# Moving the sums and splits of GpSimd to VectorE in a fused attention and two-network kernel, with the gate as one ScalarE function and the pair stages in a written-out order

## The chip, the cores and the metric

The kernel runs on one core of one Trainium2 chip. The metric is the device time of one execution in microseconds, as the median of three runs. Beside the runs there is one profiled execution, whose instructions are in the trace. Engines are called by their names in the profile: PE is TensorE's matmul, PEld its weight load, DVE is VectorE, ACT is ScalarE, POOL is GpSimd, SP is the engine that issues most DMAs.

## The reference

Eight batches of eight heads (576 tokens, 64 columns per head) go through a linear attention; its output is 4608 tokens of 512 columns. These go through a network with squared ReLU and then through a gated network:

```
q_s = softmax(q, last axis);  k_s = softmax(k, token axis)
x   = q_s @ (k_s^T @ v)                    (heads side by side: 4608 x 512)
h   = relu(x @ w_in) ** 2;  x = h @ w_out  (2048 hidden columns)
xn  = x / sqrt(mean(x * x) + 1e-6) * rms_g
g   = xn @ w_gate;  val = xn @ w_val       (1536 hidden columns)
out = (g * sigmoid(g) * val) @ w_out2
```

All inputs and outputs are fp32.

## The kernel before

**Precision.** A matmul operand in fp32 is held as two fp32r tiles, a high part and a low part. ACT makes the high part with a copy, another engine the low part with a subtraction (operand minus high part). A product is then three matmuls (`PASSES`: high with high, high with low, low with high). So nearly every operand costs one ACT copy and one subtraction before PE can use it.

**Blocks.** The 4608 tokens are nine blocks of 512. The first network runs block after block (j from 0 to 8), in 16 units per block: unit (j, c) makes one slice of 128 hidden columns (`p1_A`, 12 matmuls into `ps_h`), squares the ReLU on ACT and splits it (`p1_hi`, `p1_lo`, tiles `r` and `g`), and two units later adds it to the four banks `acc` (`p1_B`, 12 matmuls). Attention for the following block runs beside it: the table `todo` gives each step of a pair of heads a place in the half units (`attention(2 * i)`, `attention(2 * i + 1)`).

**Weights of the second network.** They come as 64-bit words and must be made into fp32 and into the seven operands of a Strassen-Winograd product. This is done beside blocks 2 to 7 of the first network (counted from 0). `tick()` advances a pipeline: `d_load` (DMA), `d_words` (a scaling of the upper words, tile `s`, and an ACT copy of the lower words, tile `n`), `d_float` (three DVE instructions that write tile `t12`, `t21`, `t22` or `t11`). When four such tiles are there, `d_quad` queues 4 sums (`s1` to `s4`) and 7 or 8 splits into tiles `so` in the list `outs`; one entry is taken out per unit, and a second one while more than 8 are queued. A finished `so` tile is sent to DRAM (`wd_t`, `wd_v`) by a DMA of ACT (`send`, `flush`). Tiles `t12` and `t21` have two buffers, `t22` and `t11` one; `so` has four. In the kernel before, POOL makes the scalings of these weights, the sums and the low parts of `so`.

**The second network.** Blocks 0 to 7 are taken in four pairs (a pair stage), block 8 alone. A pair stage has two phases:

- Phase A (`p2_A`): for n from 0 to 5, 14 steps of 6 matmuls (512 columns). Seven steps give the gate half (k = 0), seven the value half (k = 1), into banks `ps_x`, `ps_y`, `ps_v` and `ps_w`; `ps_x` and `ps_y` share two buffers with `ps_h` and `ps_s`. DVE adds the banks up (`u`, `silu`, `g`). In the gate half ACT takes a Sigmoid (tile `sg`) and DVE multiplies it with its argument.
- Phase V (`p2_V`): 7 products i with 6 slices n each, 42 steps of 12 matmuls (256 columns). The operand of each step is a tile `ob` (four buffers): `p2_hi` copies the high part on ACT four steps ahead, `p2_lo` makes the low part on DVE three steps ahead. Four of the seven operands are sums or differences of `g` tiles: 24 such instructions per pair stage, made by POOL in place.

`b_tasks(s + 1)` spreads the preparation of the next stage over both phases: square sums and the root mean square (`b_sq`, `b_sum`, `b_rms`, `b_inv`), the scaling (`b_xn`), the sums for Strassen (`b_t`, `b_x4`), and in phase V the splits `xo` of 14 operand tiles (`b_xh` on ACT, `b_xl` on DVE).

**What sets the order.** While `pinned[0]` is true, every engine's instructions stay in the order in which the code records them; else a scheduler may move them. Before, phase V and nearly all of the first network are recorded in this way, phase A is not. Each engine runs its queue in order, so an instruction that waits holds up all behind it.

Of the kernel before, what the change touches and what calls it, by code (L numbers as in the profile page):

```python
# [8 lines left out]
F32 = mybir.dt.float32  # L9
# [31 lines left out]
def attention_moe_kernel(  # L41
# [84 lines left out]
    NOB = 4  # L126
    X0, XN = 2, 36
    NTAG = 8
# [127 lines left out]
    def d_words(key):  # L256
        r = raws.pop(key).bitcast(U32).rearrange("p (n two) -> p n two", two=2)
        turns["d"] += 1
        s = pools["d"].tile([P, 512], F32, tag=f"s{turns['d'] % 2}", name="s", bufs=1)
        n = pools["d"].tile([P, 512], I32, tag=f"n{turns['d'] % 2}", name="n", bufs=1)  # L260
        hi = r[:, :, 1].bitcast(F32)
        if key[0] == "o":
            se.activation(out=s, in_=hi, func=AF.Copy, scale=2.0**-112)
        else:
            eng = ve if key[0] == "i" else ge
            eng.tensor_scalar(
                out=s, in0=hi, scalar1=2.0**-112, scalar2=0.0, op0=ALU.mult, op1=ALU.add
            )
        se.activation(out=n, in_=r[:, :, 0], func=AF.Copy, scale=2.0**-29)
        words[key] = s, n  # L270

    def d_float(key):
# [21 lines left out]
        floats[key] = t.bitcast(F32)  # L294

    def w_split(t, f, eng):
        se.activation(out=t[:, 0], in_=f, func=AF.Copy)
        eng.tensor_tensor(out=t[:, 1], in0=f, in1=t[:, 0].bitcast(F32), op=ALU.subtract)

# [41 lines left out]

    outs = []

    def d_out(key, f):
        def run():
            turns["so"] += 1
            t = pools["q"].tile([P, 2, 512], F32R, tag=f"so{turns['so'] % 4}", name="so", bufs=1)
            w_split(t, f(), ge)
            send(key, t, 1)

        outs.append(run)

    def d_quad(key):
        n, c = key
        if n != "11":
            return
        f = {"a" + b: floats.pop((b, c)) for b in ("11", "12", "21", "22")}

        def d_sum(name, in0, in1, op):
            def run():  # L360
                f[name] = pools["q"].tile([P, 512], F32, tag=name, name=name, bufs=1)
                ge.tensor_tensor(out=f[name], in0=f[in0], in1=f[in1], op=op)

            outs.append(run)

        def out(name):
# [12 lines left out]
        out("s2")  # L379
        out("a12")  # L380
        out("s4")
# [569 lines left out]

    x2s, sums, rinv = {}, {}, {}

# [4 lines left out]

    def b_sq(j, m0):
        x2 = x2s[j]  # L960
        for m in range(m0, m0 + 2):
            s = ep.tile([P, T], F32, tag="e", name="sq")
            se.activation(out=s, in_=x2[:, m, :], func=AF.Square)
            if m == 0:
                sums[j] = s
            else:
                a = sums[j]
                if m == 1:
                    a = pools["x"].tile([P, T], F32, tag="sa", name="sa", bufs=1)
                ve.tensor_tensor(out=a, in0=sums[j], in1=s, op=ALU.add)  # L970
                sums[j] = a

    def b_sum(j):
        a = sums.pop(j)
        t = pools["x"].tile([P, 2, T], F32R, tag="shl", name="shl", bufs=1)
        split(t, a)
        sums[j] = t

    def b_rms(j):
# [4 lines left out]
        y = pools["x"].tile([P, T], F32, tag="y", name="y", bufs=1)  # L984
        se.activation(out=y, in_=ps, func=AF.Ln, bias=eps_sb)
        se.activation(out=y, in_=y, func=AF.Exp, scale=-0.5)
        a = pools["x"].tile([P, T], F32, tag="sa", name="sa", bufs=1)
        ve.tensor_scalar_add(out=a, in0=ps, scalar1=1e-6)
        rinv[j] = (y, a)

    def b_inv(j):
        y, a = rinv[j]
        ve.tensor_tensor(out=a, in0=a, in1=y, op=ALU.mult)
        ve.tensor_tensor(out=a, in0=a, in1=y, op=ALU.mult)
        ve.tensor_scalar(
# [84 lines left out]
    def p2_A(s, n, q):  # L1080
# [63 lines left out]
        if step == 0:  # L1144
            se.activation(out=sv("p1"), in_=ps, func=AF.Copy)
        elif step == 1:
            add(sv("u2"), ps, sv2["p1"])
        elif step == 3:
            out(0, 0, ps2.pop("x"))
        elif step == 2:  # L1150
            se.activation(out=sv("p5"), in_=ps, func=AF.Copy)
        elif step == 4:
            add(sv("u3"), ps2.pop("y"), sv2["p1"])
        elif step == 5:
            out(0, 1, ps2.pop("v"), sv2["u2"])
        else:
            w = ps2.pop("w")
            out(1, 0, w, sv2["u3"])
            out(1, 1, sv2["p5"], sv2["u3"])

    gs, ops, banks, parts2 = {}, {}, {}, {}
    BSTEPS = ("b11", "t2", "b21", "t3", "t1", "t4", "b22")
    AT = {"b11": (0, 0), "b12": (0, 1), "b21": (1, 0), "b22": (1, 1)}
    AT |= {"t2": (0, 0), "t3": (0, 1), "t1": (0, 1), "t4": (1, 0)}

    def p2_g(n, name):
        k, t = AT[name]
        return gs[2 * n + k][:, t]

    def p2_hi(i, n):  # L1170
        o = ops[i, n] = pools["x"].tile([P, 2, T], F32R, tag="ob", name="ob", bufs=NOB)
        se.activation(out=o[:, 0], in_=p2_g(n, BSTEPS[i]), func=AF.Copy)

    def p2_lo(i, n):
# [5 lines left out]
        for out, in0, in1, op in {  # L1180
            "b11": (("t3", "b22", "b12", ALU.subtract), ("t2", "t3", "b11", ALU.add)),
            "b21": (("t4", "b21", "t2", ALU.subtract),),
            "t3": (("t1", "b22", "t2", ALU.subtract),),
        }.get(name, ()):
            ge.tensor_tensor(out=p2_g(n, out), in0=p2_g(n, in0), in1=p2_g(n, in1), op=op)

    def p2_V(s, i, n):
# [26 lines left out]
        def part(name, h):  # L1214
            tag = {"p1": ("p1", "u2"), "u2": ("silu10", "silu11"), "p5": ("p5", "u3")}[name][h]
            parts2[name, h] = pools["x"].tile([P, T], F32, tag=tag, name=tag, bufs=1)
            return parts2[name, h]
# [13 lines left out]
        for h in range(2):  # L1231
# [9 lines left out]
            elif i == 4:  # L1241
                se.activation(out=part("p5", h), in_=p, func=AF.Copy)
            elif i == 5:
                done(0, 1, h, lambda e: add(e, p, parts2["p1", h]))
                done(
                    1, 1, h, lambda e: add(e, parts2.pop(("p5", h)), parts2.pop(("p1", h)))
                )
            else:
# [60 lines left out]
    def b_tasks(s):  # L1309

        blocks = stages[s]
        tasks = [(0, b_load, (j,)) for j in blocks]
        at = 6
        for j in blocks:
            tasks += [(at, b_sq, (j, 0)), (at + 6, b_sq, (j, 2)), (at + 12, b_sum, (j,))]
            tasks += [(at + 16, b_rms, (j,)), (at + 19, b_inv, (j,))]
            tasks += [(at + 23 + 3 * m, b_xn, (j, m)) for m in range(KD)]
            at += 35
        tasks += [(n, b_t, (s, b)) for n, b in ((76, "b"), (76, "t1"), (79, "t2"), (82, "t3"))]
        names = [b for a, b, bank in STEPS]  # L1320
# [3 lines left out]
        for i, (b, kk) in enumerate(tiles):  # L1324
            at = NA + i if s == 0 else NA + X0 + i * XN // len(tiles)
            if b == "t4":
                tasks.append((at - 1 - 3 * kk, b_x4, (s, kk)))
            tasks += [(at, b_xh, (s, b, kk)), (at + 1, b_xl, (s, b, kk))]
        return sorted(tasks, key=lambda x: x[0])

    with ExitStack() as ctx_a:
# [127 lines left out]
        for i, (j, c) in enumerate(units):  # L1459
# [47 lines left out]
            attention(2 * i + 1)  # L1507
            if i == n1 - FF1 - 1:
                assert not outs and ticks[0] == len(jobs) + 4
# [13 lines left out]
        for op in plan2:  # L1523
# [5 lines left out]
            elif op[0] == "A":  # L1529
                _, s, n, q = op  # L1530
                p2_A(s, n, q)
                at = n * 2 * NS + q
                if n == NQ - 1 and len(stages[s]) == 2:
                    if q in (2, 4, 6, 8):
                        p2_hi(0, q // 2 - 1)
                    if q in (3, 5, 7, 9):
                        p2_lo(0, q // 2 - 1)
            else:
# [6 lines left out]
                if NOB <= at + NOB - 1 < NS * NQ:  # L1545
                    p2_lo(*divmod(at + NOB - 1, NQ))
                at += NA
            if at is not None and s + 1 < len(stages):
                for when, f, args in b_tasks(s + 1):
                    if when == at:  # L1550
                        f(*args)
                pinned[0] = False

# [44 lines left out]
```

## Time and profile before

| | |
|---|---|
| median of three runs | 1719.31 us (1718.97 to 1719.57) |
| profiled execution, its time | 1717.88 us |
| its span, first to last instruction | 1715.7 us |
| PE busy | 1683.8 us, 98% of the span |
| DVE busy | 1165.0 us, 68%, 1895 instructions |
| ACT busy | 833.1 us, 49% |
| POOL busy | 347.4 us, 20%, 271 instructions |

The span is what the trace covers; the profiled execution took 2.2 us more than it. Busy time is the union of an engine's instructions. A row of the chain or of a wait names what ended the idle time, with `<-` before the releaser. The granted TensorE clock is 1.00 in nearly all of the span.

### The profile page before, as it was taken

What the parts mean: (1) busy time and instruction counts of PE and PEld (TensorE: products, weight loads), DVE (VectorE), ACT (ScalarE), POOL (GpSimd) and SP (SyncE); (2) the same over time, 40 slices, a digit from 0 to 9 for tenths busy, and PEclk for the clock granted to TensorE, in tenths of its full rate; (3) what the DMA queues carried; (4) which work ended last, traced back from release to release, by engine and by line L of the source; (5) the groups of instructions that cost most, each with busy time, mean ns of one, the idle gap of its engine ahead of it and who ended that gap; (6) DMA issues with size and microseconds to landing.
All of it is one profiled execution on the core that took longest, in us unless ns stands there. A gap on an engine that the chain in (4) does not pass through costs nothing.

```text
span 1715.7 us, 25334 instructions
## 1 busy us (share of the span) xinstructions
PE 1683.8 (98%) x9254; PEld 1433.2 (84%) x9254; DVE 1165.0 (68%) x1895; ACT 833.1 (49%) x1454; POOL 347.4 (20%) x271
## 2 busy tenths in 40 slices
PE   7999999999999999999999999999999999999998
PEld 5788888888878778888888789888987899889997
DVE  7986556656765666432457889688978897868744
ACT  7875345555555555543555345434644354324422
POOL 4000001233442334320001114011501150214000
PEclk9999999999999999999999999999999999999999
DMA  9986666798988988675556556755585557556786
GB/s 239 306 286 240 203 188 218 243 310 263 323 297 257 304 250 276 226 246 197 172 199 206 187 194 202 252 187 193 182 272 185 196 184 246 187 194 198 248 303 221
DMA packets 202554, 398.03 MB, mean 232 GB/s; under 512 B 57664, under 2 KB 123200, under 8 KB 201280
## 3 DMA queue, kind: packets, MB, share of 16 engines
q1 hardware_dynamic: 162800, 348.97, 62.4%
q10 hardware_dynamic: 39632, 47.46, 8.0%
q8 instruction: 74, 1.21, 0.3%
q14 instruction: 48, 0.39, 0.1%
HBM read 330.30 MB, written 66.06 MB: 231 GB/s over the span
## 4 chain that ended last, share of the span: by engine, by line
PE 83%; DVE 11%; issue 3%; ACT 1%; DMA 1%; POOL 1%; ACTq 0%; SPq 0%; DVEq 0%; POOLq 0%
PE acc L34 23%; PE ps_h L34 21%; PE ps_x L34 15%; PE ps_y L34 11%; PE ps_v L34 7%; PE ps_w L34 4%; DVE ob L34 3%; DVE g L34 2%; DVE xo L34 1%; PE ps_kv L34 1%; DVE t L34 1%; DVE u L34 1%; DVE silu L34 1%; DVE sa L34 1%; DVE x L34 1%
## 5 line engine op out<-in xcount | busy, mean ns | idle before, releaser
L34 PE MATMUL ps_h<-x,ws 128*128 128x512 f32 x1296 | 315.4, 393 | 0.3 <-ACT r L34 0.3
L34 PE MATMUL acc<-g,ws 128*128 128x512 f32 x1296 | 314.0, 391 | 0.0
L34 POOL TENSOR_TENSOR g<-g 128x512 f32<-128x512 f32 x96 | 155.4, 1631 | 663.8 <-DVE g L34 411.2
L34 PEld LDWEIGHTS acc<-g,ws 128*128 128x128 f32 x1296 | 241.4, 188 | 50.0
L34 PEld LDWEIGHTS ps_h<-x,ws 128*128 128x128 f32 x1296 | 240.1, 188 | 50.7 <-ACT r L34 1.2
L34 DVE TENSOR_TENSOR g<-r,g 128x512 fp32r<-128x512 f32 x156 | 111.8, 717 | 132.4 <-ACT g L34 132.3
L34 ACT ACTIVATE r<-ps_h 128x512 f32<-128x512 f32 x144 | 85.8, 596 | 217.7 <-PE ps_h L34 214.4
L34 ACT ACTIVATE ob<-g 128x512 fp32r<-128x512 f32 x168 | 106.1, 632 | 142.4 <-PE ps_x L34 67.8
L34 PE MATMUL ps_y<-xo,ws 128*128 128x512 f32 (+1 forms) x720 | 168.5, 369 | 1.6 <-DVE u L34 1.6
L34 PE MATMUL ps_v<-xo,ws 128*128 128x512 f32 (+1 forms) x720 | 169.0, 368 | 0.0
L34 PE MATMUL ps_x<-xo,ws 128*128 128x512 f32 (+1 forms) x720 | 168.0, 369 | 0.0
L34 DVE TENSOR_TENSOR ob<-g,ob 128x512 fp32r<-128x512 f32 x168 | 145.7, 890 | 24.5 <-ACT ob L34 22.7
L34 PEld LDWEIGHTS ps_y<-xo,ws 128*128 128x128 f32 x720 | 126.6, 189 | 25.7 <-DVE u L34 3.1
L34 PEld LDWEIGHTS ps_x<-xo,ws 128*128 128x128 f32 x720 | 126.9, 189 | 23.7 <-DVE u L34 1.2
L34 PEld LDWEIGHTS ps_v<-xo,ws 128*128 128x128 f32 x720 | 127.4, 188 | 23.0
L34 PE MATMUL ps_x<-ws,ob 128*128 128x256 f32 x1152 | 142.4, 283 | 0.4
L34 PEld LDWEIGHTS ps_x<-ws,ob 128*128 128x128 f32 x1152 | 140.0, 192 | 1.9 <-DVE ob L34 1.6
L34 PE MATMUL ps_y<-ws,ob 128*128 128x256 f32 x864 | 107.4, 284 | 7.5 <-DVE ob L34 7.5
L34 PEld LDWEIGHTS ps_y<-ws,ob 128*128 128x128 f32 x864 | 104.9, 192 | 8.9 <-DVE ob L34 8.9
L34 ACT ACTIVATE g<-r 128x512 fp32r<-128x512 f32 x156 | 98.4, 631 | 22.6 <-DVE r L34 18.4
L34 PE MATMUL ps_h<-x,w 128*128 128x512 f32 x432 | 104.6, 392 | 2.1 <-DVE x L34 2.1
L34 PE MATMUL acc<-g,w 128*128 128x512 f32 x432 | 105.1, 392 | 0.0
(165 smaller groups left out, 2351.8 us busy)
## 6 DMA issues: line engine op xcount, KB each, us to landing
ws<-wd_t SPq DMA_DIRECT2D x210, 512.0 KB, 3.3
ws<-wd_o SPq DMA_DIRECT2D x96, 512.0 KB, 4.5
ws<-wd_i SPq DMA_DIRECT2D x88, 512.0 KB, 4.5
ws<-wd_v SPq DMA_DIRECT2D x84, 512.0 KB, 3.3
wd_t<-so ACTq DMA_DIRECT2D x84, 256.0 KB, 5.2
raw<-in_w_gv SPq DMA_DIRECT2D x36, 512.0 KB, 5.7
wd_v<-so ACTq DMA_DIRECT2D x48, 256.0 KB, 3.7
x2d<-e SPq DMA_DIRECT2D x36, 256.0 KB, 3.5
```

The costliest lines, as they stand in the source:

```text
L34: ins = f(*args, **kw)
```

## The change

1. `d_words`: the scaling of the second network's weights goes from POOL to DVE. `d_sum` and the low part in `d_out` likewise. The low part is no longer recorded with its copy: it goes to a list `lows`, emptied after the unit's second attention step, and its tile is sent at once. A second entry of `outs` is taken while more than 5 are queued, not 8.
2. `p2_A`: Sigmoid and multiplication become one ACT function, Silu, recorded a little later (`later`). Phase A of a pair stage is pinned.
3. `p2_lo` no longer makes the sums of `g`; a new `p2_t` makes each of them on DVE, at places written out in `V_SUMS` and in the main loop: `t3` in phase A, `t2` in phase A or in the first three steps of phase V, `t1` and `t4` in steps 14 to 26 of phase V.
4. `b_tasks`: single steps at fixed places (`V_LOWS`, `V_T4` for phase V) in the place of an even spread. In `b_rms` ACT copies the bank (plus 1e-6), which DVE did, and ACT squares the inverse root, which saves DVE one multiplication per block.
5. `p2_V`: product 4 is added to the result at once, where before ACT copied it for product 5.

```
-    X0, XN = 2, 36
+    V_SUMS = {1: (4, "t2"), 2: (5, "t2")}
+    V_SUMS |= {15 + n: (n, "t1") for n in range(6)}
+    V_SUMS |= {at: (n, "t4") for n, at in enumerate((14, 21, 22, 24, 25, 26))}
+    V_LOWS = (3, 4, 5, 6, 7, 8, 9, 10, 27, 28, 30, 31, 32, 33)
+    V_T4 = (12, 13)
...
-            eng = ve if key[0] == "i" else ge
-            eng.tensor_scalar(
+            ve.tensor_scalar(
...
-            w_split(t, f(), ge)
-            send(key, t, 1)
+            src = f()
+            se.activation(out=t[:, 0], in_=src, func=AF.Copy)
+
+            def low():
+                ve.tensor_tensor(
+                    out=t[:, 1], in0=src, in1=t[:, 0].bitcast(F32), op=ALU.subtract
+                )
+                send(key, t, 0)
+
+            lows.append(low)
...
-                ge.tensor_tensor(out=f[name], in0=f[in0], in1=f[in1], op=op)
+                ve.tensor_tensor(out=f[name], in0=f[in0], in1=f[in1], op=op)
...
-        se.activation(out=y, in_=ps, func=AF.Ln, bias=eps_sb)
+        a = pools["x"].tile([P, T], F32, tag="sa", name="sa", bufs=1)
+        se.activation(out=a, in_=ps, func=AF.Copy, bias=1e-6)
...
-                g = pools["x"].tile([P, T], F32, tag="sg", name="sg", bufs=2)[:, 0:W]
-                se.activation(out=g, in_=h, func=AF.Sigmoid)
-                ve.tensor_tensor(out=to, in0=h, in1=g, op=ALU.mult)
+                later.append(lambda: se.activation(out=to, in_=h, func=AF.Silu))
...
+    def p2_t(n, name):
+        in0, in1, op = {
+            "t3": ("b22", "b12", ALU.subtract),
+            "t2": ("t3", "b11", ALU.add),
+            "t4": ("b21", "t2", ALU.subtract),
+            "t1": ("b22", "t2", ALU.subtract),
+        }[name]
+        ve.tensor_tensor(out=p2_g(n, name), in0=p2_g(n, in0), in1=p2_g(n, in1), op=op)
...
-            ge.tensor_tensor(out=p2_g(n, out), in0=p2_g(n, in0), in1=p2_g(n, in1), op=op)
...
-            at = NA + i if s == 0 else NA + X0 + i * XN // len(tiles)
+            at = NA + (i if s == 0 else V_LOWS[i] - 1)
...
-                if len(outs) > 8:
+                if len(outs) > 5:
...
+                pinned[0] = len(stages[s]) == 2
...
+                if at in V_SUMS:
+                    p2_t(*V_SUMS[at])
```

**Place 1: DVE beside the first network, where a float tile's buffer is used again.** `t12` is the float tile of a weight, `so` the split of an older one, `g` a split of the first network, `x`, `qT`, `mk`, `mc` attention steps. Before:

```order
L34 TENSOR_REDUCE mk_6318<-kt_6038 128x128
L34 TENSOR_TENSOR mk_6318<-mk_6318,kt_6038 64x128
L34 TENSOR_TENSOR g_6314<-r_6311,g_6314 128x512
L34 TENSOR_SCALAR t12_6336<-s_6224 128x512
L34 SCALAR_TENSOR_TENSOR t12_6336<-s_6224,t12_6336 128x512
L34 ISA t12_6336<-t12_6336,n_6225 128x1024
L34 TENSOR_REDUCE mc_6384<-ps_kt_6360 128x1
```

Of the change:

```order
L34 TENSOR_TENSOR so_6244<-s2_5975,so_6244 128x512
L34 TENSOR_TENSOR g_6274<-r_6271,g_6274 128x512
L34 TENSOR_TENSOR so_6301<-t12_5314,so_6301 128x512
L34 TENSOR_TENSOR x_6305<-ps_x_6276,x_6305 128x512
L34 TENSOR_TENSOR qT_6307<-ps_q_6246,qT_6307 128x512
L34 TENSOR_REDUCE mk_6330<-kt_6044 128x128
L34 TENSOR_TENSOR mk_6330<-mk_6330,kt_6044 64x128
L34 TENSOR_TENSOR g_6326<-r_6323,g_6326 128x512
L34 TENSOR_SCALAR t12_6348<-s_6238 128x512
L34 SCALAR_TENSOR_TENSOR t12_6348<-s_6238,t12_6348 128x512
```

The last reader of the old buffer (`so` from `t12`) was an instruction of POOL's queue; now it is one of DVE's own, six rows ahead of the instruction that writes the buffer again.

**Place 2: DVE in phase V of the first pair stage, from the third product on.** `ob` is a low part that PE waits for, `xo` a low part for the next stage, `t` a sum for the next stage, `g` a sum of this stage, `p` and `u` are sums that empty banks. Before:

```order
L34 TENSOR_TENSOR ob<-g,ob 128x512 x3
L34 TENSOR_TENSOR xo<-t_9717,xo 128x512
L34 TENSOR_TENSOR ob<-g,ob 128x512 x2
L34 TENSOR_TENSOR xo<-t_9717,xo 128x512
L34 TENSOR_TENSOR ob<-g,ob 128x512 x3
L34 TENSOR_TENSOR xo<-x_8783,xo 128x512
L34 TENSOR_TENSOR ob<-g,ob 128x512 x3
L34 TENSOR_TENSOR xo<-x_8783,xo 128x512
```

Of the change:

```order
L34 TENSOR_TENSOR t_9641<-x_8785,t_9641 128x512
L34 TENSOR_TENSOR ob<-g,ob 128x512
L34 TENSOR_TENSOR t_9641<-x_8785,t_9641 128x512
L34 TENSOR_TENSOR ob<-g,ob 128x512
L34 TENSOR_TENSOR g<-g 128x512
L34 TENSOR_TENSOR ob<-g,ob 128x512
L34 TENSOR_TENSOR g<-g 128x512
L34 TENSOR_TENSOR ob<-g,ob 128x512
L34 TENSOR_TENSOR g<-g 128x512
```

The sums `g<-g`, which stood in POOL's queue, now stand in DVE's, one between each two low parts; the splits `xo` have moved to other steps.

## Rows read from the trace of the kernel before

**Rows 1.** The page, part 1: busy time and instructions of each engine.

```profile
PE 1683.8 (98%) x9254; PEld 1433.2 (84%) x9254; DVE 1165.0 (68%) x1895; ACT 833.1 (49%) x1454; POOL 347.4 (20%) x271
```

**Rows 2.** PE's waits: us in total, times, longest us.

```profile
PE ps_y L34 <- DVE ob L34: 7.5, 7, 1.6
...
PE ps_kt L34 <- DVE mk L34: 2.5, 4, 0.9
...
PE ps_h L34 <- DVE x L34: 2.1, 1, 2.1
PE ps_y L34 <- DVE u L34: 1.6, 3, 0.6
PE acc L34 <- ACT g L34: 1.3, 1, 1.3
PE ps_x L34 <- DVE qT L34: 1.0, 1, 1.0
...
PE ps_kb L34 <- DVE x L34: 0.4, 1, 0.4
```

**Rows 3.** All engines' waits (same columns), two of the first network.

```profile
POOL so L34 <- ACT so L34: 248.2, 46, 12.5
...
DVE t L34 <- POOL so L34: 26.0, 6, 8.8
```

**Rows 4.** Timeline (start us, us, instruction, [idle before]), first network, around 609 us.

```profile
607.27 0.62 ACT L34 ACTIVATE so<-t 128x512 fp32r<-128x512 f32 x1
...
608.03 1.29 POOL L34 TENSOR_TENSOR so<-t,so 128x512 fp32r<-128x512 f32 x1 [4.96 <-ACT so L34]
...
609.35 1.50 DVE L34 TENSOR_SCALAR t<-s 128x512 uint32<-128x512 uint32 x1 [7.77 <-POOL so L34]
...
615.98 0.68 DVE L34 TENSOR_TENSOR x<-ps_x,x 128x512 fp32r<-128x512 f32 x1
...
616.71 0.73 PE L34 MATMUL ps_h<-x,w 128*128 128x512 f32 x2 [2.08 <-DVE x L34]
```

**Rows 5.** Timeline of PE in the first phase V.

```profile
1014.98 8.79 PE L34 MATMUL ps_x<-ws,ob 128*128 128x256 f32 x72
1023.61 8.80 PE L34 MATMUL ps_y<-ws,ob 128*128 128x256 f32 x72
...
1043.58 4.58 PE L34 MATMUL ps_y<-ws,ob 128*128 128x256 f32 x36 [0.85 <-DVE ob L34]
1049.26 2.90 PE L34 MATMUL ps_y<-ws,ob 128*128 128x256 f32 x22 [1.11 <-DVE ob L34]
...
1078.56 1.55 PE L34 MATMUL ps_x<-xo,ws 128*128 128x512 f32 x6
```

**Rows 6.** Timeline of DVE and POOL in the same phase V.

```profile
1028.01 0.68 DVE L34 TENSOR_TENSOR xo<-t,xo 128x512 fp32r<-128x512 f32 x1
...
1033.89 5.08 POOL L34 TENSOR_TENSOR g<-g 128x512 f32<-128x512 f32 x3 [0.71 <-DVE ob L34]
...
1036.04 1.78 DVE L34 TENSOR_TENSOR xo<-t,xo 128x512 fp32r<-128x512 f32 x1
```

**Rows 7.** DVE's groups by form: count | busy us, mean ns | idle before.

```profile
L34 DVE TENSOR_TENSOR ob<-g,ob 128x512 fp32r<-128x512 f32 x168 | 145.7, 890 | 24.5 <-ACT ob L34 22.7
...
L34 DVE TENSOR_TENSOR silu<-silu,sg 128x512 f32<-128x512 f32 x72 | 48.4, 685 | 7.1 <-ACT sg L34 6.9
...
L34 DVE TENSOR_SCALAR s<-raw 128x512 f32<-128x512 f32 x16 | 6.7, 419 | 0.0
```

**Rows 8.** POOL's costliest groups by form.

```profile
L34 POOL TENSOR_TENSOR g<-g 128x512 f32<-128x512 f32 x96 | 155.4, 1631 | 663.8 <-DVE g L34 411.2 <-PE ps_x L34 147.2 <-DVE ob L34 103.7
L34 POOL TENSOR_TENSOR so<-s,so 128x512 fp32r<-128x512 f32 x36 | 49.3, 1370 | 150.5 <-ACT so L34 126.4 <-issue 10.8 <-DVE t L34 7.6
```

**Rows 9.** Busy us of each engine in the first phase V (PE, PEld, DVE, ACT, POOL).

```profile
1015.00:1078.50 63.50, 61.41 (x505) 60.60 (x504) 54.69 (x67) 35.39 (x60) 24.43 (x15) 1.00 0.63 212
```

More of the change, by code (lines that the diff above doesn't have):

```diff
@@ L294, in d_float @@
         floats[key] = t.bitcast(F32)
-    def w_split(t, f, eng):
-        se.activation(out=t[:, 0], in_=f, func=AF.Copy)
-        eng.tensor_tensor(out=t[:, 1], in0=f, in1=t[:, 0].bitcast(F32), op=ALU.subtract)
     late = []
@@ L339, in d_lo @@
             send(key, t, 1)
-    outs = []
+    outs, lows = [], []
     def d_out(key, f):
@@ L949, in p1_out @@
             nc.sync.dma_start(out=x2d[j][:, m, :], in_=e)
-    x2s, sums, rinv = {}, {}, {}
+    x2s, sums, rinv, sqs = {}, {}, {}, {}
     def b_load(j):
@@ L957, in b_load, with b_sq, b_add, b_shi @@
         x2s[j] = t
[L959 to L974, printed above, removed]
-        t = pools["x"].tile([P, 2, T], F32R, tag="shl", name="shl", bufs=1)
-        split(t, a)
+    def b_sq(j, m):
+        t = sqs[j, m] = ep.tile([P, T], F32, tag="e", name="sq")
+        se.activation(out=t, in_=x2s[j][:, m, :], func=AF.Square)
+    def b_add(j, m):
+        a = sqs.pop((j, 0)) if m == 1 else sums[j]
+        t = pools["x"].tile([P, T], F32, tag="sa", name="sa", bufs=1) if m == 1 else a
+        ve.tensor_tensor(out=t, in0=a, in1=sqs.pop((j, m)), op=ALU.add)
+        sums[j] = t
+    def b_shi(j):
+        t = pools["x"].tile([P, 2, T], F32R, tag="shl", name="shl", bufs=1)
+        se.activation(out=t[:, 0], in_=sums[j], func=AF.Copy)
+        sums[j] = t, sums[j]
+    def b_slo(j):
+        t, a = sums[j]
+        ve.tensor_tensor(out=t[:, 1], in0=a, in1=t[:, 0].bitcast(F32), op=ALU.subtract)
         sums[j] = t
@@ L984, in b_rms, with b_ln, b_exp @@
         y = pools["x"].tile([P, T], F32, tag="y", name="y", bufs=1)
-        se.activation(out=y, in_=ps, func=AF.Ln, bias=eps_sb)
+        a = pools["x"].tile([P, T], F32, tag="sa", name="sa", bufs=1)
+        se.activation(out=a, in_=ps, func=AF.Copy, bias=1e-6)
+        rinv[j] = (y, a)
+    def b_ln(j):
+        y, a = rinv[j]
+        se.activation(out=y, in_=a, func=AF.Ln)
+    def b_exp(j):
+        y, a = rinv[j]
         se.activation(out=y, in_=y, func=AF.Exp, scale=-0.5)
-        a = pools["x"].tile([P, T], F32, tag="sa", name="sa", bufs=1)
-        ve.tensor_scalar_add(out=a, in0=ps, scalar1=1e-6)
-        rinv[j] = (y, a)
+        z = ep.tile([P, T], F32, tag="e", name="z")
+        se.activation(out=z, in_=y, func=AF.Square)
+        rinv[j] = (y, a, z)
     def b_inv(j):
-        y, a = rinv[j]
-        ve.tensor_tensor(out=a, in0=a, in1=y, op=ALU.mult)
-        ve.tensor_tensor(out=a, in0=a, in1=y, op=ALU.mult)
+        y, a, z = rinv[j]
+        ve.tensor_tensor(out=a, in0=a, in1=z, op=ALU.mult)
         ve.tensor_scalar(
@@ L1145, in p2_A @@
             se.activation(out=sv("p1"), in_=ps, func=AF.Copy)
+            while later:
+                later.pop(0)()
         elif step == 1:
@@ L1149, in p2_A @@
             out(0, 0, ps2.pop("x"))
+            while later:
+                later.pop(0)()
         elif step == 2:
@@ L1155, in p2_A @@
             out(0, 1, ps2.pop("v"), sv2["u2"])
+            while later:
+                later.pop(0)()
         else:
@@ L1161, in attention_moe_kernel @@
     gs, ops, banks, parts2 = {}, {}, {}, {}
+    later = []
     BSTEPS = ("b11", "t2", "b21", "t3", "t1", "t4", "b22")
@@ L1179, in p2_lo @@
         )
[L1180 to L1184, printed above, removed]
-            ge.tensor_tensor(out=p2_g(n, out), in0=p2_g(n, in0), in1=p2_g(n, in1), op=op)
     def p2_V(s, i, n):
@@ L1214, in part @@
         def part(name, h):
[L1215 removed]
+            tag = {"p1": ("p1", "u2"), "u2": ("silu10", "silu11")}[name][h]
             parts2[name, h] = pools["x"].tile([P, T], F32, tag=tag, name=tag, bufs=1)
@@ L1241, in p2_V @@
             elif i == 4:
-                se.activation(out=part("p5", h), in_=p, func=AF.Copy)
+                done(1, 1, h, lambda e: add(e, p, parts2["p1", h]))
             elif i == 5:
[L1244 to L1247, printed above, removed]
+                done(0, 1, h, lambda e: add(e, p, parts2.pop(("p1", h))))
             else:
@@ L1312, in b_tasks @@
         tasks = [(0, b_load, (j,)) for j in blocks]
[L1313 to L1319, printed above, removed]
+        for at, j in zip((9, 37), blocks):
+            tasks += [(at + n, b_sq, (j, m)) for m, n in enumerate((0, 1, 2, 3))]
+            tasks += [(at + 1 + m, b_add, (j, m)) for m in (1, 2, 3)]
+            tasks += [(at + 6, b_shi, (j,)), (at + 7, b_slo, (j,)), (at + 10, b_rms, (j,))]
+            tasks += [(at + 14, b_ln, (j,)), (at + 15, b_exp, (j,)), (at + 20, b_inv, (j,))]
+            tasks += [(at + 22 + 2 * m, b_xn, (j, m)) for m in range(KD)]
+        tasks += [(n, b_t, (s, b)) for n, b in ((66, "b"), (66, "t1"), (72, "t2"), (77, "t3"))]
         names = [b for a, b, bank in STEPS]
@@ L1324, in b_tasks @@
         for i, (b, kk) in enumerate(tiles):
-            at = NA + i if s == 0 else NA + X0 + i * XN // len(tiles)
+            at = NA + (i if s == 0 else V_LOWS[i] - 1)
             if b == "t4":
-                tasks.append((at - 1 - 3 * kk, b_x4, (s, kk)))
+                tasks.append((at - 1 - 3 * kk if s == 0 else NA + V_T4[kk], b_x4, (s, kk)))
             tasks += [(at, b_xh, (s, b, kk)), (at + 1, b_xl, (s, b, kk))]
@@ L1507, in attention_moe_kernel @@
             attention(2 * i + 1)
+            while lows:
+                lows.pop(0)()
             if i == n1 - FF1 - 1:
@@ L1530, in attention_moe_kernel @@
                 _, s, n, q = op
+                pinned[0] = len(stages[s]) == 2
                 p2_A(s, n, q)
                 at = n * 2 * NS + q
[L1533 to L1537, printed above, removed]
+                if len(stages[s]) == 2 and (n > 0 and q == 5 or n == NQ - 1 and q == 2 * NS - 1):
+                    p2_t(n - (q == 5), "t3")
+                if len(stages[s]) == 2:
+                    for k in range(NOB):
+                        when = at - (NQ - 3 + k // 2) * 2 * NS - 9 - k % 2
+                        if when == 0:
+                            p2_hi(0, k)
+                        elif when == 1:
+                            p2_lo(0, k)
+                        elif when == 3:
+                            p2_t(k, "t2")
             else:
@@ L1551, in attention_moe_kernel @@
                         f(*args)
-                pinned[0] = False
+            pinned[0] = False
 def kernel(**inputs):
```

## The prediction

> **What bounds the kernel now.** I read the busy times of the engines first: PE is busy in 98% of the span, DVE in 68%, POOL in 20% [rows 1]. The matmuls themselves are the same before and after, so the change can only take away what is left beside them, the time in which PE waits. So the next view is the list of PE's waits. After the first 60 us it has three kinds, and that list is the whole stock [rows 2]:
>
> - beside the first network, waits for attention steps of DVE: `mk` 2.5 us, `x` 2.1 and 0.4, `qT` 1.0, together 6.0;
> - in phase A of the pair stages, 1.6 us for DVE's `u`, which empties a bank;
> - in phase V, 7.5 us in 7 waits for DVE's `ob`.
>
> The wait of 1.3 us for ACT at the end belongs to the single last stage and stays. Each of the three kinds names DVE, so the third view is what held DVE up. There are two answers.
>
> The first is a wait. In the list of all waits DVE stands before its instruction `t` for POOL's `so`, 6 times, 26.0 us in all [rows 3]. The timeline shows one of them link by link [rows 4]: ACT copies `so` at 607.27, POOL makes the low part at 608.03, DVE, which had nothing to do for 7.77 us, starts `t` at 609.35, its attention step `x` comes at 615.98, and PE, which needs it, has lost 2.08 us.
>
> The second is slow instructions. In phase V the same DVE instruction `xo` takes 0.68 us at 1028.01 and 1.78 us at 1036.04, inside a run of three POOL sums that lasts 5.08 us [rows 6]. A gate multiplication, made where POOL is idle, takes 685 ns in the mean; `ob`, of the same size, takes 890 [rows 7].
>
> In phase V the price of this can be read in full. Six steps (72 matmuls) start 8.63 us after the six before them (1014.98 to 1023.61), so 42 steps would take 7 times 8.63, or 60.4 us; the phase takes 63.6 (1014.98 to 1078.56) [rows 5]. So 3.2 us are lost, of which the two marked waits are 1.96: a wait costs about 1.6 times what its row shows, since PE restarts slowly and shorter waits follow.
>
> **The change part by part.**
>
> *Phase V.* DVE's work there, counted in the order: 38 low parts, 14 splits for the next stage, 14 sums that were POOL's, 2 `b_x4` and 8 instructions that empty banks, 76 in all. At 685 ns [rows 7] they are 52.1 us of the 60.4, though no longer in the company of POOL. A step lasts 8.63 / 6 = 1.44 us, and the written-out order puts two DVE instructions (1.37 us) in a step and three (2.06) in the four steps where DVE empties banks. A low part has three steps, 4.3 us, before PE needs it, and ACT's copy takes under one of them, so 0.6 us of delay in one step is covered, and is worked off in the next ones. If that cover is gone, each late `ob` costs PE what it is late. I count the waits as gone: between 7.5 (the rows alone) and 1.6 times 7.5 = 12. I take 11, near the upper end, because the phase whose loss was read in full gave the factor.
>
> *Phase A.* The three waits for `u` [rows 2] go with the slow instructions ahead of it: 1.6 us. The Silu takes one DVE multiplication away per gate tile and is one ACT function where Sigmoid was one, so ACT gets nothing from it; DVE loses 96 multiplications of 685 ns (65.8 us) and 24 of half the width. Beside that, DVE gets 10 of the 24 sums of each pair stage, in a phase that is more than 110 us long. ACT gains a copy and a squaring per block and stands at 49% [rows 1]: I cost both at nothing, covered by ACT's idle half, and if not, a late `p` copy would hold `u` and then the bank. Bounds: 0 to 1.6 times 1.6 = 2.6; I take 1.6.
>
> *First network.* Moved to DVE: 66 low parts and 36 sums at 685 ns, 36 scalings at 419 ns, 85 us. From the order: the low part that reads the old `t12` is now in DVE's own queue ahead of the instruction that overwrites it, so `t` no longer waits for POOL, and the earlier emptying of `outs` moves ACT's copies ahead too. What is late next is ACT's copy: a low part still waits for it, and behind it stands the next attention step. The six holds, 26.0 us, cost PE 6.0, that is 0.23 us per us of hold. I take that a sixth of this stays as waits for ACT: 5.0 of the 6.0 are gained. Bounds: nothing to 1.6 times 6.0 = 9.6.
>
> *DVE as a whole.* Added: 198 instructions at 685 ns and 36 at 419, 150.7 us. Removed: the gate's 65.8 and some 10 for the half-wide ones, and 18 instructions of the mean square, 12.3; together 88. Given back by `ob` alone, 168 times (890 - 685) ns = 34.4. So DVE would end at about 1165 + 151 - 88 - 34 = 1194 us, 70%, or less where other groups get faster too. POOL, at 1.63 and 1.37 us for each of what it gives up [rows 8], falls from 347.4 to its early work; by what is left of its queue I put that at 25 us, an estimate.
>
> *The DMAs* of `so` go out one unit earlier, on the same queue (ACT), 132 of them as before; SP's queue keeps its order but for a few places. At nothing: no wait of PE's for a DMA is in the list after the start.
>
> The sum: 11 + 1.6 + 5.0 = 17.6 us off 1717.88 of the profiled execution gives 1700.3. The median of the runs stands 1.4 us above that execution, so I forecast **1701.7 us**, 1.0% less.
>
> **The rivals.**
>
> *All of it.* The 1.6 applies everywhere and no new wait appears: 12 + 2.6 + 9.6 = 24 would be the end; with 11 + 2.6 + 7 = 20.6 it is 1699. For it: the order was written step by step around these waits. Against it: DVE is as full in phase V as before. 0.17.
>
> *Phase V and A only.* In the first network ACT's copies hold DVE as POOL's low parts did. For it: the six holds began with a late ACT copy (607.27), POOL's part is only 1.3 us at its end [rows 4]. Against it: the copy itself comes earlier in the queue. Gain 12.6: 1706.7. 0.18.
>
> *DVE becomes the bound of phase V.* DVE is busy 54.69 of 63.50 us there [rows 9]. If these are its own time and not POOL's doing, 14 sums of 685 ns make it 64.3, 0.7 us more than the phase lasts now: 4 times 0.7 lost, 6.6 gained elsewhere, 1715.5. The rows speak against it: 0.68 and 1.78 us for one instruction [rows 6]. The Trainium skill ("Perfetto Trace Analysis", Optimizing Scalar/DVE Operations) says that where DVE is saturated, work may be moved off it, even to GpSimd; the change does the reverse. By that rule the sums belong where they were, and the time is this rival's. The same section adds that both share a read port of SBUF, so that moving between the two might not help; the trace agrees with the second sentence. 0.12.
>
> *Slower: DVE waits for ACT as POOL did.* POOL waited 248.2 us in 46 waits for ACT's copy of `so` [rows 3], 5.4 us each, and nobody stood behind it. Now 66 low parts make that wait on DVE, in order, with attention behind them. At 0.23 us of PE per us of hold, the 12.6 us gained in the second network are used up when the holds reach 55 us, 0.83 per low part. If a third of POOL's waiting, 83 us, falls on DVE, PE loses 19 and the time is 1719.3 - 12.6 + 19 = 1726. Against it: the low part is recorded after the next attention step, by which time the copy (0.62 us) is mostly done, and DVE would be idle in part of these waits anyway. 0.08.
>
> **How the numbers follow.** The forecast has 0.45, its own range 1699.5 to 1704.5. A measurement can tell 0.2%, 3.4 us, from no change: faster is below 1715.9, slower above 1722.7. The forecast, the first two rivals and most of the third lie below: 0.87. Within: 0.06. Slower: 0.07. The range goes from 1697 (all of it, with room for the bounds) to 1712, and leaves out most of the third rival and the slower one, together under 0.2.
>
> **What would show it.** In the profile after: PE's waits for `ob` and `u` gone, the three together under 3 us after the start; no wait of DVE's `t` for another engine, and small ones of `so` for ACT; `ob` near 690 ns; phase V at 60.5 to 61 us; POOL near 25 us; DVE at 65 to 70%. If DVE's `so` waits for ACT for over 30 us in all, or PE's waits for attention steps are still over 4 us, the term of the first network is wrong. If `ob` is still over 800 ns without POOL, the reading of the slow instructions is wrong.

## The result and the profile after

The changed kernel takes **1695.62 us** (median of four runs, 1695.02 to 1695.87), the kernel before 1719.14 (four runs): a ratio of 0.9863, 95% interval 0.9845 to 0.9880. That is 23.5 us less, where 17.6 were forecast; the time lies 1.4 us below the low end of the range, 1697.

The page of the changed kernel, part 1 (busy time and instructions of each engine), against [rows 1]:

```profile
PE 1677.3 (99%) x9254; PEld 1434.4 (85%) x9254; DVE 1121.7 (66%) x1991; ACT 831.0 (49%) x1461; POOL 20.1 (1%) x37
```

From the list of its waits, the three longest of PE, which answer to [rows 2], and DVE's for ACT's `so` and `s` (us in total, times, longest):

```profile
PE ps_kt L34 <- DMA kt<-in_k: 5.0, 1, 5.0
...
PE ps_kb L34 <- ACT ek L34: 2.2, 4, 1.6
...
PE acc L34 <- ACT g L34: 1.3, 1, 1.3
...
DVE so L34 <- ACT so L34: 0.8, 2, 0.4
...
DVE t L34 <- ACT s L34: 0.5, 1, 0.5
```

Every wait of PE for `mk`, `x`, `qT`, `u` and `ob` is gone. What is left stands in the first 60 us (`kt`, `ek`) and at the end (`acc`). DVE's `t` waits for POOL no more, and the low parts, now DVE's own, wait 0.8 us for ACT in all.

DVE's groups by form (count | busy us, mean ns | idle before), against [rows 7]:

```profile
L34 DVE TENSOR_TENSOR ob<-g,ob 128x512 fp32r<-128x512 f32 x168 | 114.1, 688 | 13.1 <-ACT ob L34 9.8
...
L34 DVE TENSOR_TENSOR g<-g 128x512 f32<-128x512 f32 x96 | 66.0, 687 | 1.2
```

The timeline of PE in the first phase V, against [rows 5]: seven products of 72 matmuls, 8.64 us apart, with no gap.

```profile
1005.66 8.80 PE L34 MATMUL ps_x<-ws,ob 128*128 128x256 f32 x72
1014.29 8.80 PE L34 MATMUL ps_y<-ws,ob 128*128 128x256 f32 x72
...
1057.49 8.80 PE L34 MATMUL ps_x<-ws,ob 128*128 128x256 f32 x72
1066.13 1.55 PE L34 MATMUL ps_x<-xo,ws 128*128 128x512 f32 x6
```

**Where the time went.** PE runs the same 9254 matmuls in both kernels, so the start of one and the same matmul can be compared. I cut the program at five kinds of places: the 111th matmul into `ps_h` (end of "start"), the 1426th of 1728 (end of "first network"; the rest of that network lasts 143.47 us in every kernel), the first `ps_x<-xo` of each stage (phase A begins), the first `ps_x<-ws` (phase V begins), and the first matmul of the last unit into `acc` (end of "last stage"). Each number is the difference of two such starts ("start" counts from the beginning of the span); of the four pair stages the table shows the second. The kernels below the first two are those of the experiments.

| us | start | first network | phase A | phase V | last stage | median |
|---|---|---|---|---|---|---|
| before | 77.91 | 671.58 | 116.53 | 63.60 | 92.18 | 1719.14 |
| after | 77.22 | 664.05 | 115.55 | 60.47 | 92.17 | 1695.62 |
| e1 sums on GpSimd | 77.51 | 664.07 | 115.45 | 61.15 | 92.21 | 1696.63 |
| e2 before, sums on VectorE | 77.16 | 672.63 | 115.49 | 60.47 | 92.17 | 1703.73 |
| e3 low parts on GpSimd | 78.36 | 664.07 | 115.51 | 60.47 | 92.17 | 1694.65 |
| e4 scalings, sums on GpSimd | 77.50 | 664.06 | 115.51 | 60.47 | 92.17 | 1695.22 |
| e5 both of these | 77.68 | 664.05 | 115.53 | 60.47 | 92.17 | 1694.85 |
| e6 before, limit 5 | 77.33 | 664.06 | 116.56 | 63.59 | 92.17 | 1709.74 |
| e7 before, low parts listed | 77.21 | 674.18 | 116.57 | 63.59 | 92.17 | 1719.90 |
| e8 Sigmoid and multiplication | 77.60 | 664.06 | 118.73 | 60.47 | 92.17 | 1706.51 |
| e9 before, two edits | 77.66 | 664.07 | 115.49 | 60.47 | 92.19 | 1695.53 |
| e10 after, one unit held | 76.95 | 664.05 | 115.55 | 60.47 | 90.61 | 1693.57 |
| e11 two edits, one unit held | 77.60 | 664.05 | 115.51 | 60.47 | 90.61 | 1693.99 |
| e12 multiplication later | 77.84 | 664.04 | 115.71 | 60.47 | 92.17 | 1695.94 |

Over all stages the change gives 0.69 us in the start, 7.53 in the first network, 3.43 in the four phases A (1.09, 0.98, 1.00, 0.36) and 11.21 in the four phases V (3.11, 3.13, 3.13, 1.84): 22.86, as the two profiled executions differ (1717.88 and 1695.02). The start is not the change's: it varies from 76.95 to 78.36 among kernels whose code is the same there.

### The profile page after: what moved, and what is told of

Read it like the earlier page. It is cut to its first block, busy times and chain, and to the rows that moved or that the text cites. A ratio compares the mean times of both kernels' runs of the same rounds, so it can differ in the third digit from the quotient of the medians.

```text
span 1692.7 us, 25216 instructions
## 1 busy us (share of the span) xinstructions
PE 1677.3 (99%) x9254; PEld 1434.4 (85%) x9254; DVE 1121.7 (66%) x1991; ACT 831.0 (49%) x1461; POOL 20.1 (1%) x37
## 4 chain that ended last, share of the span: by engine, by line
PE 97%; DVE 1%; DMA 1%; ACT 0%; issue 0%; SPq 0%; POOLq 0%; ACTq 0%; DVEq 0%
PE acc L34 25%; PE ps_h L34 23%; PE ps_x L34 18%; PE ps_y L34 15%; PE ps_v L34 9%; PE ps_w L34 4%; PE ps_kv L34 1%; PE ps_q L34 1%; DVE t L34 1%; DMA vs<-in_v 0%; PE ps_kt L34 0%; PE ps_kb L34 0%; PE ps_s L34 0%; DMA kt<-in_k 0%; DVE m L34 0%
## 5 line engine op out<-in xcount | busy, mean ns | idle before, releaser
L34 DVE TENSOR_TENSOR g<-r,g 128x512 fp32r<-128x512 f32 x156 | 107.1, 686 | 112.4 <-ACT g L34 112.2
L34 DVE TENSOR_TENSOR u<-ps_y,p 128x512 f32<-128x512 f32 (+1 forms) x120 | 76.4, 637 | 109.7 <-PE ps_y L34 86.0
L34 PEld LDWEIGHTS ps_y<-xo,ws 128*128 128x128 f32 x720 | 127.0, 189 | 23.5 <-DVE u L34 1.2
L34 DVE TENSOR_TENSOR ob<-g,ob 128x512 fp32r<-128x512 f32 x168 | 114.1, 688 | 13.1 <-ACT ob L34 9.8
```

What stands on the lines that cost most here:

```text
L34: ins = f(*args, **kw)
```

## The experiments

### Phase V: the engine of the sums, or their places

e1 takes the changed kernel and puts the 24 sums of each pair stage back on GpSimd; e2 takes the kernel before and changes the one word the other way.

```diff
 e1, in p2_t of the changed kernel
-        ve.tensor_tensor(out=p2_g(n, name), ...)
+        ge.tensor_tensor(out=p2_g(n, name), ...)
 e2, in p2_lo of the kernel before
-            ge.tensor_tensor(out=p2_g(n, out), ...)
+            ve.tensor_tensor(out=p2_g(n, out), ...)
```

> The changed kernel with one thing undone: the 24 sums of each pair stage are made by GpSimd again, at the places where the change wrote them. Theory C (company: DVE's instructions with two SBUF operands get slow while GpSimd works, whatever the order): ob over 850 ns in the mean instead of 688, phase V of the first three pair stages 62.5 us or more instead of 60.4, total 1704 to 1708. Theory O (order: the gain of phase V comes from the places that are written out, not from the engine): phase V at most 60.8, total at most 1697.

> The kernel before with one word changed: the same 24 sums on VectorE, at their old places behind the low parts. Theory C: ob falls to about 690 ns, phase V to 60.5 to 61 us, PE's seven waits for ob are gone, total 1719.1 - 11 = 1708, or 1706.5 if phase A's waits for u go as well. Theory O: DVE, with two sums bunched behind one low part, still makes PE wait for ob, 2 us or more in each of three stages; total 1715 or above.

Measured: e1 1696.63 us (ratio 0.9869, 0.9854 to 0.9885), e2 1703.73 (0.9911, 0.9895 to 0.9926). In e2 it is as C says, and the total is lower still; in e1 neither theory holds. DVE's `ob` and PE's wait for it in e1:

```profile
L34 DVE TENSOR_TENSOR ob<-g,ob 128x512 fp32r<-128x512 f32 x168 | 163.0, 992 | 14.1 <-ACT ob L34 12.4
```

```profile
PE ps_y L34 <- DVE ob L34: 1.3, 3, 0.4
```

With GpSimd at work among DVE's instructions `ob` is slower in the mean than before the change (992 ns, against 890 in [rows 7]), as C says; but phase V is only 0.68 us longer than in the changed kernel, not 3.1. One late operand is left in each of the first three phases V, and the timeline shows it:

```profile
1049.12 3.28 PE L34 MATMUL ps_y<-ws,ob 128*128 128x256 f32 x26
1052.83 5.77 PE L34 MATMUL ps_y<-ws,ob 128*128 128x256 f32 x46 [0.43 <-DVE ob L34]
```

In e2 the sums stand where they always stood, `ob` takes 687 ns, and phase V lasts 60.47 us, with no loss at all:

```profile
L34 DVE TENSOR_TENSOR ob<-g,ob 128x512 fp32r<-128x512 f32 x168 | 113.8, 687 | 22.4 <-ACT ob L34 20.9
```

So the full loss of 3.1 us needs both, the slow instructions and the old places. To take away the slowness is enough; the new places alone are enough for four fifths (2.45 of 3.13 us).

It is not that the sums are spread out in time. GpSimd makes 15 of them in the first phase V both in the kernel before and in e1, and in e1, where each has a step of its own in the order, eight run end to end:

```profile
1034.92 13.70 POOL L34 TENSOR_TENSOR g<-g 128x512 f32<-128x512 f32 x8 [0.62 <-DVE ob L34]
```

What differs is what DVE has to do beside them. The kernel before, then e1:

```profile
1041.75 4.07 DVE L34 TENSOR_TENSOR ob<-g,ob 128x512 fp32r<-128x512 f32 x3
1045.74 1.78 DVE L34 TENSOR_TENSOR xo<-x,xo 128x512 fp32r<-128x512 f32 x1
1047.44 4.07 DVE L34 TENSOR_TENSOR ob<-g,ob 128x512 fp32r<-128x512 f32 x3
```

```profile
1041.68 7.49 DVE L34 TENSOR_TENSOR ob<-g,ob 128x512 fp32r<-128x512 f32 x5
```

Before, a slow split `xo` for the next stage stands behind three low parts, and DVE needs 1.9 us per operand (5.69 from one three to the next) where PE takes one each 1.44. In e1 the change has moved the splits out of this stretch, and DVE needs 1.5. This points at the places of the splits more than at those of the sums, but no run moves one without the other.

In phase A, too, either is enough: in e2, without the Silu and without a written order, it is as short as in the changed kernel (115.49), and so it is in e1 with GpSimd's sums (115.45).

### The first network: which of its edits

e3, e4 and e5 put work of the changed kernel back on GpSimd; e6 and e7 take one half of the new order into the kernel before.

```diff
 e3, in d_out
-                ve.tensor_tensor(out=t[:, 1], in0=src, ...)
+                ge.tensor_tensor(out=t[:, 1], in0=src, ...)
 e4, in d_words and d_sum
-            ve.tensor_scalar(out=s, in0=hi, ...)
+            (ve if key[0] == "i" else ge).tensor_scalar(out=s, in0=hi, ...)
-                ve.tensor_tensor(out=f[name], ...)
+                ge.tensor_tensor(out=f[name], ...)
 e5: e3 and e4
 e6, in the kernel before
-                if len(outs) > 8:
+                if len(outs) > 5:
 e7, in the kernel before: the low part goes to the list lows (on ge),
 emptied behind attention(2 * i + 1), and its tile is sent at once
```

> The changed kernel with the 66 low parts of so made by GpSimd, at the same place of the program. Theory W (the first network's loss was DVE's t standing in order behind GpSimd's low part): t waits 15 us or more for so again, PE loses 5 to 7.5 us before block 6, total 1701 to 1703. Theory S (the loss was DVE's instructions getting slow beside GpSimd): PE loses 1 to 3 us there, in proportion to GpSimd's busy time, and t waits for so under 5 us; total 1697 to 1699.

> The changed kernel with the 36 scalings s and the 36 sums of the first network on GpSimd, and the low parts left on VectorE. Theory W: no wait of t for so comes back, PE's loss beside the first network stays under 1 us, total 1695 to 1697. Theory S: DVE's t, x and qn instructions beside GpSimd take over 1000 ns, PE loses 3 us or more there; total 1698.5 or above.

Measured: e3 1694.65 (0.9857, 0.9840 to 0.9875), e4 1695.22 (0.9862, 0.9846 to 0.9878), with the first network at 664.07 and 664.06. W expected e3 to bring the loss back, and it didn't: `t` has no wait for `so` there. S falls as well. So in the new order the engine of these instructions makes no difference, unless either relief alone was enough; that was the next question.

> The changed kernel with all of the first network's moved work (scalings, sums, low parts) on GpSimd again, its new order kept (at most 5 waiting entries, low parts listed behind the attention steps, sent at once). Theory Q (what healed the first network is the new order, not the engine): the stretch from block 0 to block 6 lasts 664 to 665 us as in the changed kernel (before 671.6), total 1695 to 1697. Theory E (either engine's relief was enough, since with low parts alone or scalings and sums alone on GpSimd the loss stayed away): with all three on GpSimd the stretch is 669 us or longer, t waits 10 us or more for so, total 1700 to 1704.

> The kernel before with the limit of the list of splits at 5 instead of 8, nothing else. Theory Q1 (of the new order the earlier emptying counts): the first network's stretch falls from 671.6 to 664 or 666 us, total 1712 to 1713.5. Theory Q2 (what counts is that the low parts are listed behind the attention steps): the stretch stays at 669 to 672 us, total 1717 to 1720.

> The kernel before with the low parts, still on GpSimd, listed and made behind the second attention step of the unit and sent at once, the limit left at 8. Theory Q1: the first network's stretch stays at 669 to 672 us, since the low part only comes later for the t that waits for it; total 1717 to 1721. Theory Q2: it falls to 664 to 666 us, total 1712 to 1713.5.

Measured: e5 1694.85 (0.9860, 0.9846 to 0.9875); e6 1709.74 (0.9947, 0.9930 to 0.9963); e7 1719.90 (1.0005, 0.9996 to 1.0014). E falls with e5, Q2 with e7. Q1 holds for the stretch, though e6's total is 2.3 us below its range: one digit in the kernel before shortens the first network from 671.58 to 664.06, the whole gain of the stretch. The timeline of e6, ACT and POOL and then DVE, at the place of [rows 4]:

```profile
588.75 0.61 ACT L34 ACTIVATE so<-t 128x512 fp32r<-128x512 f32 x1
...
589.50 1.28 POOL L34 TENSOR_TENSOR so<-t,so 128x512 fp32r<-128x512 f32 x1 [2.31 <-DMA qt<-in_q]
```

```profile
596.81 0.68 DVE L34 TENSOR_TENSOR g<-r,g 128x512 fp32r<-128x512 f32 x1
597.41 0.41 DVE L34 TENSOR_SCALAR t<-s 128x512 uint32<-128x512 uint32 x1
597.86 1.74 DVE L34 SCALAR_TENSOR_TENSOR t<-s,t 128x512 uint32<-128x512 uint32 x1
```

At this place e6 runs 4.08 us ahead of the kernel before. There DVE was free for this `t` at 609.35 - 7.77 = 601.58, and ACT copied the last `so` that reads the old tile at 607.27. In e6 the same `t` comes up at 597.41 (601.49 in the other's time), and the same copy was made at 588.75 (592.83), 14.4 us earlier; GpSimd's low part was done at 590.78, 6.6 us before `t`. The wait for GpSimd was mostly a wait for the list. In e7 the listing takes nothing away: DVE's row of waits is that of [rows 3] to the digit.

```profile
DVE t L34 <- POOL so L34: 26.0, 6, 8.8
```

In e7's first network 1.6 us of the 2.6 more, and the 1.05 us more in e2's, come from the clock (last section); e7's other 1.0 us is a standstill of PE near 668 us, where `x` is late as well. Not run was the opposite of e5, the kernel before with these instructions on VectorE and the limit left at 8. [rows 4] lets one expect little gain from it, since ACT's copy at 607.27 would have been as late, but that isn't shown.

### The gate

e8 undoes the Silu in the changed kernel; e12 does too, but records DVE's multiplication one step later, behind that step's own instructions.

```diff
 e8, in p2_A, run where the Silu was
-                later.append(lambda: se.activation(out=to, in_=h, func=AF.Silu))
+                se.activation(out=g, in_=h, func=AF.Sigmoid)
+                ve.tensor_tensor(out=to, in0=h, in1=g, op=ALU.mult)
 e12: the multiplication goes to a list that is emptied at the end of the next step
```

> The changed kernel with the gate made by Sigmoid and VectorE's multiplication again, in the places of the Silu. Theory N (phase A's loss came from GpSimd's sums beside VectorE and from the places of the sums, as the runs with one of the two undone gained it all; the Silu gives nothing): phases A of the pair stages last 115.4 to 115.7 us as in the changed kernel, total 1695 to 1697. Theory L (VectorE's load in phase A counts): they last 116 us or more, PE waits for u again, total 1697.5 to 1699.

> The changed kernel with Sigmoid and multiplication again, but VectorE's multiplication put one step later (behind the next step's own instructions). Theory I (with the gate undone, phase A lost 3.2 us a stage because VectorE stood in order behind ACT's Sigmoid, with u queued behind it): phases A return to 115.5 to 116 us, total 1696 to 1698, silu's waits for sg fall from 72.5 to under 20 us. Theory L (VectorE's load with 96 more multiplications): they stay above 118 us, total above 1704.

Measured: e8 1706.51 (0.9928, 0.9913 to 0.9943): phase A 118.73, longer than before the change. N falls, and it is more than L expected; e12 parts L from I: with all 96 multiplications in it, 1695.94 (0.9864, 0.9849 to 0.9879), phase A 115.71. The waits in e8, then in e12:

```profile
DVE silu L34 <- ACT sg L34: 72.5, 81, 5.3
...
PE ps_y L34 <- DVE u L34: 7.8, 13, 0.9
```

```profile
DVE silu L34 <- ACT sg L34: 18.6, 12, 3.2
...
PE ps_y L34 <- DVE u L34: 0.3, 2, 0.2
```

In e8's timeline the multiplications that come right behind their Sigmoid stand ahead of `u`, which empties the bank that PE waits for:

```profile
942.52 1.29 DVE L34 TENSOR_TENSOR silu<-silu,sg 128x512 f32<-128x512 f32 x2 [0.16 <-ACT sg L34]
...
943.73 0.75 DVE L34 SCALAR_TENSOR_TENSOR x<-x,g_sb,y 128x512 f32<-128x512 f32 x1
944.39 0.69 DVE L34 TENSOR_TENSOR u<-ps_y,p 128x512 f32<-128x512 f32 x1
...
945.13 1.66 PE L34 MATMUL ps_y<-xo,ws 128*128 128x512 f32 x6 [0.88 <-DVE u L34]
```

So the Silu is worth 10.9 us against a Sigmoid with its multiplication written at the same place, and nothing that can be measured against one written a step later. How much of e8's loss is DVE's waiting for ACT and how much the two multiplications in a row, the two runs don't part.

### Two edits, and one unit held back

e9 puts the word of e2 and the digit of e6 into the kernel before. e10 changes the plan of the changed kernel, so that in the last of the six rounds (n = 5) of the single last stage unit 9 of the last product runs after the last gate product; e11 does both.

```diff
 e10 and e11, in make_plan
-                    if q % NS in (2, 4):
+                    if q % NS in (2, 4) and (pair or n < NQ - 1 or q == 2):
                         more(1)
```

> The kernel before with two edits: the 24 sums of each pair stage on VectorE (one word) and the limit of the list of splits at 5 (one digit). Theory T (these two carry everything; the other moves, the Silu and the written-out steps add nothing): the gains of the two single runs add up, 15.3 - 0.3 (noise of the start and one dip of the clock) and 9.4 less a start of 0.6, so 1695 to 1697; first network 664.1 us, phases V 60.47, phases A 115.5. Theory R (the rest of the change is worth something of its own): 1698 or above.

> The changed kernel with one unit of the last product held back: in the last quarter of the single last stage, unit 9's twelve matmuls run after the last gate product instead of beside it, so that they cover the wait of 1.27 us of PE for ACT's g. If that wait is free to be covered: the last stage falls from 92.17 to about 90.8 us, total 1694.2 against 1695.6. If the tail behind it (the copies and the transfers out) or g's buffers decide: 92.1 or above, total unchanged.

> Both of the above on the kernel before: two edits and the held unit. If they are independent: 1694 to 1695.5, and as fast as the changed kernel with the held unit within 1 us. If the order that the scheduler finds around the held unit differs: 1696 or above.

Measured: e9 1695.53 us (0.9862, 0.9847 to 0.9877), T holds: word and digit together give as much as the whole change. e10 1693.57 (0.9851, 0.9834 to 0.9867) and e11 1693.99 (0.9852, 0.9837 to 0.9866): the last stage is 1.56 us shorter, the wait of 1.27 and PE's restart behind it. PE's end in the changed kernel, then in e10:

```profile
1680.54 0.88 PE L34 MATMUL ps_w<-xo,ws 128*128 128x256 f32 x6
1682.69 5.74 PE L34 MATMUL acc<-ws,g 128*128 128x512 f32 x24 [1.27 <-ACT g L34]
```

```profile
1677.53 0.88 PE L34 MATMUL ps_w<-xo,ws 128*128 128x256 f32 x6
1678.25 8.35 PE L34 MATMUL acc<-ws,g 128*128 128x512 f32 x36
```

e10's runs (1693.20 to 1693.98) all lie below the changed kernel's; e10 and e11, whose runs overlap, are the fastest kernels here.

## Why the prediction was right and wrong

**Right.** The places of the loss were read rightly: the time came out of the three stretches in which PE waited on DVE, nothing appeared in their place, and each of the three kinds of wait went. Phase V was put at 11 and gave 11.21. That a wait costs more than its row held there; that 11 was so near is in part luck, since it was chosen between 7.5 and 12, and the factor came out at 1.49, not 1.6 (the last pair stage lost 1.84 us where the others lost 3.1). Of what was to be seen after, `ob` near 690 ns (688), phase V at 60.5 to 61 (60.47), POOL near 25 us (20.1) and DVE at 65 to 70% (66%) are as written. The slower rival, DVE held by ACT's `so` as POOL was, priced at 1726, is refuted by the trace: 0.8 us of such waits, where 55 were needed. The rival in which DVE bounds phase V, 1715.5, is refuted too: DVE has its 14 sums more, and PE has no gap. "Phase V and A only", 1706.7, falls, though it had the cause of the six holds right: a late copy of ACT's. "All of it", 1699, came nearest. The Trainium skill ("Perfetto Trace Analysis", Optimizing Scalar/DVE Operations) says that work may be moved off a saturated DVE, even to GpSimd; by that the sums would have stayed off DVE. Here e2, which only puts them back on DVE, is 15.3 us faster than the kernel before. The same section's other sentence, that moving work between the two might not help since they share a read port, is the one that e1's 992 ns fits.

**Wrong, in two terms of the sum and in the range.**

- *First network, 5.0: measured 7.53.* The step that failed is "I take that a sixth of this stays as waits for ACT". Nothing stayed. And the 6.0 us of the rows were counted at their face, though phase V had just shown that a wait costs more: here 7.53 / 6.0 = 1.26 times. The cause was named as one of two, the low part in DVE's own queue and the earlier emptying of `outs`; e6 shows that the second is enough alone, and e5 that the first adds nothing to it. The 85 us of work that DVE took over there neither gained nor cost in the new order: the stretch is 664.05 with it and without it.
- *Phase A, 1.6: measured 3.43,* above the bound of 2.6 that was set. The step that failed is to take the list of waits for the whole stock. In the kernel before, the second phase A loses 0.98 us. The wait for `u` is 0.54 us of it by its row and 0.81 from start to start (0.58 and 0.85 in the first phase A); the rest are five starts that are late by 0.04 to 0.11 us, around `ps_s` and at bank changes, less 0.26 that the changed kernel loses near the end of the phase, and no row of waits shows any of this. It is seen only in the start-to-start times.
- *The range.* The upper bounds of the three terms, 12 + 2.6 + 9.6, made 24.2, which is 1695.1; the low end was put at 1697 nevertheless, by the rival "all of it", which had been priced at 20.6. The measured 22.9 lies inside the bounds of the terms and outside the range.

The forecast missed by 6.1 us; the three terms make 4.6 of it. The remaining 1.5 are the start (0.69, which varies from run to run) and the distance of the profiled execution to the median, taken as 1.4 before and measured as 0.6 after.

**Right in size, wrong in cause.** The slow `ob` was given as the reason of phase V's loss. It is half of one: e1 has slower ones and loses a fifth. And the Silu, which got no term of its own ("ACT gets nothing from it"), is worth nothing only beside a multiplication that doesn't stand ahead of `u`; in the pinned order, with the multiplication at the Silu's place, the time is 10.9 us longer.

DVE's total was put at 1194 us and is 1121.7: only `ob` was counted among what gets faster without POOL, where other groups did as well (`xo<-x,xo` from 1017 to 686 ns).

## What to carry to other kernels

A wait that names an engine need not be that engine's fault: look at how long ago its own input could have been there. Here GpSimd's 1.3 us stood behind a list that was emptied too late, and a digit was enough where 138 instructions had been moved. When a change has several parts that could each explain a gain, put each alone into the old kernel and take each alone out of the new one: in phase V either part was nearly enough, which neither test alone would have shown. And price a wait by the length of its stretch against the pace of the undisturbed pieces, since rows of waits show only part of it; what is missing goes by the number of waits (next section), so a factor read in one stretch needn't hold in another.

## What the runs showed of the hardware

**The clock can fall after a short wait, in some executions.** In the profiled executions of e2 and e7, behind the wait of 2.1 us for `x` that the kernel before has too, PE's clock fell. The windows of e2 (us, busy of PE, PEld, DVE, ACT and POOL with counts, granted clock, DMA share, GB/s), the same stretch of the program before, during and after:

```profile
610.00:617.00 7.00, 4.91 (x21) 3.56 (x19) 6.86 (x9) 1.38 (x3) 4.47 (x3) 0.94 0.94 297
617.00:620.00 3.00, 3.00 (x10) 2.23 (x9) 3.00 (x7) 2.19 (x4) 0.00 (x0) 0.58 0.02 6
620.00:626.00 6.00, 6.00 (x29) 4.91 (x28) 2.61 (x7) 3.34 (x8) 3.16 (x3) 1.00 0.47 137
```

For some 3 us the granted clock is 0.58 in the mean, that is mostly the lower level of 1.2 GHz; before it PE had stood still for the 2.1 us. Matmuls there start 0.43 us apart instead of 0.23, which costs e2 1.0 us and e7 1.6. In the profiled execution of the kernel before the same wait left the clock at 1.00. It is a further price of a wait that no row of the waits carries, and no profiled execution of a kernel that lacks this wait paid it (all of these have a first network of 664.04 to 664.07 us). The mean clocks of the executions without a trace suggest that in the kernel before the fall is the rule: of those of that kernel that were timed beside the experiments, 18 have 0.999 and a median of 1719.2 us, 8 have 1.00 and 1718.1 (one of 3399.96 us isn't counted). That isn't proof, since a fall at the very end of an execution lowers the mean as well (5 of the 44 executions of the kernels without the wait have 0.999). If it is so, about 1 us of the 23.5 comes from the clock.

**A wait costs PE more than its row, by a nearly fixed amount.** In phase V of the kernel before matmuls start 0.12 us apart. The one that waited 0.85 us by its row, at 1043.58, started 1.13 us after the one ahead of it, and the next one 0.22 us later: 1.11 us lost. So it is with the 1.11 (1.37 lost) and with the 1.56 of the last pair stage (1.82): 0.26 us more than the row each time. In the first network the seven waits of 6.0 us cost 7.53, 0.22 each on top. Each of the first three phases V has two more late operands of 0.03 and 0.10 us of idle time that are in no row and cost 0.29 and 0.36.

**Slow is not late.** One DVE subtraction of 128x512 takes 688 ns without GpSimd's sums, 890 in the mean with them in the old order, 992 with them in the new one, and the last of these loses PE less than the second.
